# Scores and transposes of the first groups through eight PSUM banks, a third query buffer, and a new order for an attention kernel with two layers behind it

## The chip, the cores and the metric

One core of one Trainium2 chip. The time is device microseconds (us) of one execution, the median of several. Beside it stands the span of a profiled execution, from its first to its last instruction. Engines: PE is TensorE (PEld its weight loads), DVE VectorE, ACT ScalarE, POOL GpSimd, SP the engine that issues DMAs.

## The reference, cut to what matters

```python
def _attn_ref(q, k, v, n_sink, window):          # (2, 8, 768, 64) float32, n_sink 4, window 128
    scores = scale * np.matmul(q, k.transpose(0, 1, 3, 2))
    keep = is_sink | in_window                   # 4 first keys, and the last 128
    scores = np.where(keep, scores, -1000000000.0)
    a = np.exp(scores - np.max(scores, axis=-1, keepdims=True))
    a = a / (np.sum(a, axis=-1, keepdims=True) + 1e-09)
    return np.matmul(a, v)

x = attention as (1536, 512)
h = x @ w_in                                     # (512, 2048)
g = np.where(h > 0.0, h, np.exp(np.minimum(h, 0.0)) - 1.0)
x = g @ w_out                                    # (2048, 512)
h = x @ w2_in
g = h - np.tanh(h)
return g @ w2_out
```

## The kernel before

**Order.** The program is first written down as a list of operations with their dependences (class `Plan`), then `schedule` (line 269) simulates the engines with modelled costs and picks for each engine a fixed order; `emit` issues it (line 400, which is the line that nearly all instructions show; line 168 is the same for bundles of matmuls). What an engine takes next is set by a rank: for kinds of operations in the table `DUE`, a due time that is linear in a counter; else the length of the path to the end. `PICK` says for kinds of elementwise operations which engines may do them. `BONUS` makes PE prefer to stay in its tiling mode, `MARGIN` lets an operation wait for a faster engine. When the model finds PE without work, before the first matmul of an output step, it puts in filler matmuls on constants (line 591), which keep PE running and compute nothing.

**Attention.** 12 chunks of 128 queries (6 per batch), each in two groups of 4 heads, so 24 groups g. Per group: `scores` twice, each a bundle of matmuls for two heads into two PSUM banks of `b_sc` (banks 0, 1); DVE reads each bank, adds the mask, and writes the scores and their least value (CUSTOM_DVE_ANT_0), ACT takes the exponential and the sum. `norm`: DVE adds 1e-9 and inverts, then four multiplications of 128, 256 or 264 columns (first chunk of a batch, second, others) on the engine that `PICK` says. `sink_T` and `pair_T` transpose on PE into `b_tu` (banks 2, 3), and a copy brings the result to SBUF. After two groups `PV` multiplies by the values into a bank of `b_tu` and writes x as a sum of two float32r parts, `xhi` and `xlo`. A ring of `AB = 3` buffers holds the scores of three groups, one of `QB = 2` the queries of two chunks, and `NS = 3` slots the keys.

**Layers.** Each weight tile is read as float64, narrowed by integer operations on ACT, DVE and POOL (`narrow`: absolute value, a min/max, a shift, two bit operations), and split in two float32r parts. Eight weight tiles are held. Phase 0 runs over 6 blocks of 256 tokens with 3 weight tiles: `mlp_in` (12 matmuls into a bank of `b_hA`, banks 4, 5), an elementwise part, `mlp_out` (banks 6, 7 of `b_yA`). Phase 0 runs beside the attention, as the blocks of x come. The five later phases work with 512 columns and all eight banks, when the attention is over.

**Dependences on banks.** A later user of a PSUM bank waits for the earlier ones in the order of the list; the list has all of the attention first, then the layers' steps.

Of the kernel before, what the change touches and what calls it, by code (L numbers as in the profile page):

```python
# [7 lines left out]
F32 = mybir.dt.float32  # L8
# [8 lines left out]
P = 128  # L17
# [24 lines left out]
class Plan:  # L42
# [13 lines left out]
    TOP = 640e3  # L56
    WINDOW, ENOUGH, IDLE = 3413.3, 3100.0, (109.2, 256.0)
    SWITCH = (196.0, 95.0)
    BONUS, MARGIN = 2030.75, 5520.33

    HOLD = {}
    DUE = {
# [4 lines left out]
    }  # L67

    PICK = {
        ("T", "copy", 128, True): ("ACT",), ("ew", "copy", 256, False): ("ACT", "DVE"),  # L70
        ("norm", "tensor_scalar", 264, False): ("DVE",), ("T", "copy", 64, False): ("POOL",),
        ("late w", "tensor_scalar", 512, False): ("DVE",), ("late ew", "tensor_tensor", 512, False): ("DVE",),
        ("T", "tensor_tensor", 32, False): ("DVE",), ("late ew", "copy", 512, False): ("ACT",),
        ("c", "tensor_copy", 128, False): ("POOL",), ("w", "tensor_scalar", 512, False): ("POOL",),
        ("late w", "tensor_tensor", 512, False): ("DVE",), ("late out", "copy", 512, True): ("DVE",),
        ("w", "tensor_tensor", 512, False): ("DVE",), ("T", "copy", 256, True): ("ACT",),
        ("late w", "copy", 512, False): ("DVE",), ("T", "copy", 512, True): ("ACT",),
        ("out", "copy", 512, True): ("ACT",), ("x", "copy", 512, True): ("ACT", "DVE"),
        ("norm", "tensor_scalar", 128, False): ("DVE",), ("norm", "tensor_scalar", 256, False): ("DVE", "POOL"),
        ("w", "copy", 512, False): ("ACT", "DVE", "POOL"), ("z", "copy", 512, False): ("DVE",),  # L80
        ("ew", "tensor_tensor", 256, False): ("DVE",),
    }

    def __init__(self, tc):
# [75 lines left out]
    def many(self, products):  # L160

        if self.live:
            raise AssertionError
        eng = self.T.eng

        def real():
            for kw in products:
                eng.matmul(**kw)  # L168

        mode, = {self.tiling(kw) for kw in products}  # L170
        cost = sum(self.matmul_cost(kw) for kw in products)
        work = sum(self.work_of(kw) for kw in products)
        ins, outs = [], []
        for kw in products:
            ins += [kw["lhsT"], kw["rhs"]]
            outs.append(kw["out"])
        self.enter({"PE": (cost, real, False)}, ins, outs, (), {}, "PE", False, work, mode)

    def either(self, *recs, **kw):

        if self.live:
            return getattr(recs[0][0].eng, recs[0][1])(**kw)
        cols = 1
        for k in kw["out"].shape[1:]:
            cols *= k
        psum = any(getattr(a, "space", None) == PSUM for a in kw.values())
        key = (self.tag[0], recs[1][1], cols, psum)
        pick = self.PICK.get(key)
        self.choice = key
        self.record([(r.key, m, getattr(r.eng, m)) for r, m in recs if pick is None or r.key in pick], (), kw, True)  # L190
        self.choice = None

    choice = None
# [1 line left out]
    def record(self, ways, args, kw, any_=False):  # L195
        named = list(kw.items()) + [("out" if i == 0 else f"in{i}", a) for i, a in enumerate(args)]
        named = [(k, a) for k, a in named if hasattr(a, "tensor")]
        outs = [a for k, a in named if k in ("out", "accum_out")]
        ins = [a for k, a in named if k not in ("out", "accum_out")]
        there = [a for a in ins if "DRAM" not in str(a.space)]  # L200
        eng = ways[0][0]
        costs = {}
        psum = any(a.space == PSUM for a in there + outs)
        for e, method, real in ways:
            if e == "DMA":
                size = 1
                for k in outs[0].shape[1:]:
                    size *= k
                costs[e] = (max(600.0, 0.0111 * size * outs[0].shape[0]), real, False)
            else:  # L210

                lock = (e == "DVE" and not psum) or (e == "POOL" and method == "tensor_tensor")
                costs[e] = (self.cost(e, method, outs[0], there, kw), real, lock)
        pe = eng == "PE"
        self.enter(costs, there, outs, args, kw, eng, any_, self.work_of(kw) if pe else 0.0, self.tiling(kw) if pe else 0)
# [53 lines left out]
    def schedule(self):  # L269
        from bisect import insort  # L270
        from heapq import heappush, heappop
        ops, N, engs = self.ops, len(self.ops), self.ENGINES
        succ, rank = self.ranks()
        ways = [list(o[1].items()) for o in ops]
        left = [len(o[2]) for o in ops]
        free = dict.fromkeys(engs, self.START)
        wait = {e: [] for e in engs}
# [10 lines left out]

        def offer(n):
            for k, (e, _) in enumerate(ways[n]):  # L290
                heappush(wait[e], (at[n][e] + late[n], 3 * n + k))

        for n in range(N):
            if not left[n]:
                offer(n)
        order = []
        stop, tiled, count = False, 0, 0
        win = [self.WINDOW, 2.0, 0.0, 0.0]

        def clock(t):  # L300
# [11 lines left out]
        while count < N:  # L312
# [21 lines left out]
            if e == "PE":  # L334
                top = -1e18
                for i, (v, q) in enumerate(r[:40]):
                    v = -v + (self.BONUS if ops[q // 3][7] == tiled else 0.0)
                    if v > top + 1e-9:
                        top, pick = v, i
            elif e in held:  # L340

                until = held[other[e]]
                for i, (v, q) in enumerate(r):
                    if until <= t or not ways[q // 3][q % 3][1][2]:
                        pick = i
                        break
                else:
                    s = max(t, until)
# [2 lines left out]
            c, real, lock = ways[n][q % 3][1]  # L351
            earlier = False
            for f, (cf, _, lf) in ways[n]:
                if f != e:
                    sf = max(free[f], at[n][f] + late[n])
                    if lf:
                        sf = max(sf, held[other[f]])
                    earlier = earlier or sf + cf + self.MARGIN < s + c
            if earlier:
# [5 lines left out]
            if e == "PE":  # L365

                stop = stop or (ops[n][5] or "-")[0] == "out"
                while not stop and free[e] + clock(free[e]) * self.IDLE[0] <= t:
                    order.append((free[e], -1, self.idle))
                    free[e] += run(free[e], *self.IDLE)  # L370
                    tiled = 0
                s = max(s, free[e])
                x = 0.0
                if ops[n][7] != tiled:
                    x = (self.SWITCH[1] if tiled else 0.0) + (self.SWITCH[0] if ops[n][7] else 0.0)
                    tiled = ops[n][7]
                c = run(s, c + x, ops[n][6])
            free[e] = s + c
            if lock:
                held[e] = s + c  # L380
            order.append((s, n, real))
            for k in succ[n]:
                for f in at[k]:
# [20 lines left out]
def tile_sink_attention__two_mlps(  # L404
# [119 lines left out]

    gsA = Ring("att", (2, 256), F32R, 3)

    KS, NS, QB, VB, AB, TB = 144, 3, 2, 4, 3, 8
    r_q = Ring("att", (HP, P), F32, QB)
    slots = carve("att", (NS, HP, KS))
    r_a = Ring("att", (4, KW), F32, AB)  # L530
# [14 lines left out]
    t1s += [carve("late", (DM,), U32) for _ in range(3)]  # L545
    eB, gsB = Ring("late", (512,), F32, 3), Ring("late", (2, 512), F32R, 2)
    b_sc, b_tu, b_hA, b_yA = Banks(0, 1), Banks(2, 3), Banks(4, 5), Banks(6, 7)
    b_hB, b_hE, b_yB = Banks(0, 1, 2, 3), Banks(0, 1, 2), Banks(4, 5, 6, 7)
    small = const.tile([P, 16], F32, name="small")

# [118 lines left out]
    def split_sinks(b, r):  # L669

        if b == 0:
            vsink[0] = r_vsink()
        z = vsink[b] = vsink[0]
        copy(z[0:3 * S4], r[0:3 * S4])
        rows = slice(2 * S4, 3 * S4)
        sub(V_, z[rows], r[rows], z[rows].bitcast(F32))

    a_t, aT_t, aS_t = {}, {}, {}

# [8 lines left out]
    def scores(g, pr):  # L688
# [7 lines left out]
        n = width(i)  # L696
        mm, S = [], []
        for rows in (top, bot):
            bk = b_sc(512)
            S.append(bk)  # L700
            if i == 0:
                K, to = slots[rows, o, p, 0:P], bk[:, 0:P]
# [33 lines left out]
    def sink_T(g):  # L736
# [5 lines left out]
        s = r_as()  # L742
        copy(s[:, 1:3], a.unsqueeze(1).to_broadcast([P, 2, 4, MAXSINK]))
        sub(None, s[:, 0], a, s[:, 1].bitcast(F32))
        tr = b_tu(P)[0:3 * S4]
        T_.matmul(
            out=tr, lhsT=s.rearrange("p a h s -> p (a h s)").bitcast(F32), rhs=ident,
            is_transpose=True, start=True, stop=True,
# [4 lines left out]
    def pair_T(g, pr):  # L753
# [2 lines left out]
        c = g // 2  # L756
        i = c % NI
        a = a_t[g]
        tr = b_tu(2, 2, P)
        c0, c1 = slice(0, P), slice(P, 2 * P) if i == 1 else s1  # L760
        cols = (c1, c0) if i != 1 and c % NS == 0 else (c0, c1)
        n0 = 1 if i == 0 else 0
# [8 lines left out]
    def PV(c):  # L771

        plan.tag = ("pv", 2 * c + 1)
        b, i = divmod(c, NI)
        U = b_tu(4, P)
        if i >= 2:

            plan.many([
# [412 lines left out]
```

## Time and profile before

| what | us |
|---|---|
| median of 3 runs | 637.05 (636.72 to 637.23) |
| the profiled execution | 636.36 |
| its span | 634.6 |
| PE busy, share of the span | 627.1, 99% |
| DVE busy | 431.9, 68% |
| ACT busy | 278.6, 44% |
| POOL busy | 30.8, 5% |
| granted TensorE clock, mean | 0.998 |

Busy time of PE includes the filler matmuls. Busy shares are means over stages that differ: DVE's 68% is nearly full in the first quarter and half idle later. The profiled execution took 636.36 us, 1.8 us more than its span, and 0.7 us less than the median.

### The profile page before, as it was taken

How to read it: one execution, taken by the hardware profiler on the slowest of the kernel's cores; microseconds unless marked ns; L12 is line 12 of the kernel's file. 1: busy time of each engine (PE TensorE's matmuls, PEld its weight loads, DVE VectorE, ACT ScalarE, POOL GpSimd, SP SyncE). 2: the span in 40 equal slices, each digit the busy share in tenths (PEclk: the TensorE clock that was granted, in tenths of full speed). 3: DMA queues.
4: the chain of work that ended last, by engine and by line, in shares of the span. 5: the costliest groups of instructions: out<-in, count | busy, mean ns of one | idle time of the engine just before them, and what ended most of it. 6: DMA issues, size and time to landing. Idle time of an engine off the chain costs nothing.

```text
span 634.6 us, 9256 instructions
## 1 busy us (share of the span) xinstructions
PE 627.1 (99%) x3430; PEld 514.5 (81%) x3430; DVE 431.9 (68%) x1061; ACT 278.6 (44%) x615; POOL 30.8 (5%) x41
## 2 busy tenths in 40 slices
PE   9999999999999999999999999999999999999996
PEld 6677877899888888888888888888888888888885
DVE  6999999999824479943459998367974553423232
ACT  5788887875533345533445453223422222222220
POOL 3631020100000000000000000000000000000000
PEclk9999999999999999999999999999999999999999
DMA  6543444345500122430012243011220000001012
GB/s 212 172 162 121 130 162 133 99 139 165 165 1 0 35 66 68 132 100 0 1 34 67 74 158 116 17 40 59 70 66 2 2 0 1 0 1 66 2 66 72
DMA packets 22005, 47.21 MB, mean 74 GB/s; under 512 B 2240, under 2 KB 9408, under 8 KB 21952
## 3 DMA queue, kind: packets, MB, share of 16 engines
q1 hardware_dynamic: 21952, 46.54, 23.7%
q8 instruction: 29, 0.48, 0.3%
q14 instruction: 24, 0.20, 0.1%
HBM read 43.39 MB, written 3.15 MB: 73 GB/s over the span
## 4 chain that ended last, share of the span: by engine, by line
PE 82%; DVE 13%; DMA 2%; POOL 1%; SPq 1%; issue 1%; ACT 0%; DVEq 0%; POOLq 0%
PE bank L400 79%; DVE arena L400 7%; DVE t L400 3%; PE bank L168 2%; DVE arena_r L400 1%; DVE w L400 1%; DMA raw<-in_moe_w_in_dram 1%; DVE xlo L400 1%; SPq L400 1%; POOL t L400 1%; DMA arena<-in_kq_dram 1%; DVE sm_all L400 1%; POOL arena_r L400 0%; DVE xhi L400 0%; ACT arena L400 0%
## 5 line engine op out<-in xcount | busy, mean ns | idle before, releaser
L400 PE MATMUL bank<-xhi,w 128*128 128x512 f32 (+1 forms) x840 | 250.7, 373 | 0.0
L400 PEld LDWEIGHTS bank<-xhi,w 128*128 128x128 f32 x840 | 154.6, 188 | 28.7 <-issue 1.6
L400 PE MATMUL bank<-arena_r,w 128*128 128x512 f32 (+1 forms) x684 | 158.8, 358 | 0.0
L400 PE MATMUL bank<-w,arena_r 128*128 128x512 f32 (+1 forms) x594 | 154.4, 383 | 0.0
L400 PE MATMUL bank<-xlo,w 128*128 128x512 f32 (+1 forms) x420 | 148.2, 373 | 0.0
L400 ACT CAST arena_r<-arena 128x512 fp32r<-128x512 f32 (+1 forms) x96 | 57.9, 603 | 194.2 <-PE bank L400 192.1
L400 PEld LDWEIGHTS bank<-arena_r,w 128*128 128x128 f32 x684 | 116.5, 189 | 19.3 <-issue 0.9
L400 DVE TENSOR_TENSOR arena_r<-arena,arena_r 128x512 fp32r<-128x512 f32 (+3 forms) x123 | 71.4, 582 | 89.1 <-PE bank L400 42.8
L400 PEld LDWEIGHTS bank<-w,arena_r 128*128 128x128 f32 x594 | 109.3, 188 | 22.1
L400 ACT ACTIVATE arena<-bank 128x512 f32<-128x512 f32 (+1 forms) x105 | 57.9, 560 | 101.0 <-PE bank L400 97.5
L400 PEld LDWEIGHTS bank<-xlo,w 128*128 128x128 f32 x420 | 79.0, 188 | 14.6 <-issue 1.1
L400 DVE TENSOR_TENSOR arena<-bank,arena 128x512 f32<-128x512 f32 (+1 forms) x65 | 42.4, 677 | 38.2 <-ACT arena L400 31.8
L168 PE MATMUL bank<-arena 128*64 128x128 f32 (+3 forms) x544 | 55.3, 327 | 0.5 <-DVE nm_all L400 0.4
L400 ACT ACTIVATE arena<-arena,nm_all 128x264 f32<-128x264 f32 (+2 forms) x96 | 46.8, 491 | 15.6 <-DVE nm_all L400 14.9
L400 DVE SCALAR_TENSOR_TENSOR arena<-arena,bank 128x512 f32<-128x512 f32 (+1 forms) x57 | 33.9, 596 | 22.0 <-ACT arena L400 22.0
L400 ACT ACTIVATE arena<-arena 128x512 f32<-128x512 f32 (+1 forms) x73 | 42.5, 587 | 8.1 <-DVE w L400 6.6
L168 PEld LDWEIGHTS bank<-arena 128*64 128x64 f32 (+1 forms) x544 | 34.7, 154 | 11.1 <-issue 4.3
L400 DVE SCALAR_TENSOR_TENSOR t<-raw,t 128x512 uint32<-128x512 uint32 x54 | 37.2, 688 | 0.2
L400 DVE CUSTOM_DVE_ANT_0 arena<-bank,arena 128x264 f32<-128x264 f32 (+2 forms) x96 | 35.1, 398 | 0.4 <-PE bank L168 0.2
L400 ACT COPY arena<-bank 128x512 f32<-128x512 f32 (+1 forms) x52 | 27.5, 544 | 3.2 <-PE bank L168 3.2
L400 DVE TENSOR_SCALAR t<-t 128x512 f32<-128x512 f32 (+1 forms) x64 | 27.1, 425 | 2.0 <-POOL t L400 1.1
L168 PE MATMUL bank<-ident,arena 128*128 128x128 f32 x176 | 27.6, 281 | 0.2 <-DVE xlo L400 0.2
(67 smaller groups left out, 408.8 us busy)
## 6 DMA issues: line engine op xcount, KB each, us to landing
raw<-in_moe_w_in_dram SPq DMA_DIRECT2D x20, 512.0 KB, 3.7
raw<-in_moe_w_out_dram SPq DMA_DIRECT2D x20, 512.0 KB, 3.8
arena<-in_moe_w_in_dram SPq DMA_DIRECT2D x12, 512.0 KB, 3.6
arena<-in_moe_w_out_dram SPq DMA_DIRECT2D x12, 512.0 KB, 3.6
arena<-in_kq_dram SPq DMA_DIRECT2D x22, 256.0 KB, 3.4
arena<-in_v_dram SPq DMA_DIRECT2D x12, 256.0 KB, 3.4
out_dram<-part SPq DMA_DIRECT2D x8, 256.0 KB, 2.2
out_dram<-arena SPq DMA_DIRECT2D x3, 256.0 KB, 2.5
```

What stands on the lines that cost most here:

```text
L168: eng.matmul(**kw)
L400: real(*self.ops[n][3], **self.ops[n][4])
```

## The change

Scores of the groups 0 to 5 rotate through banks 0, 1, 4, 5, and transposes and `PV` of these groups through banks 2, 3, 6. There is a third query buffer. The due times, `BONUS`, `MARGIN` and the engines in `PICK` are other ones, so the order of all engines is other. In the model of `schedule`, DVE copies and multiplications in SBUF now take up to twice as long while a POOL instruction runs beside them (the bit of `lock` worth 2). The split of the sinks (`split_sinks`) may be subtracted on POOL. `PICK` is applied within `schedule` and no longer when the operation is written down.

```diff
-    BONUS, MARGIN = 2030.75, 5520.33
+    BONUS, MARGIN = 6316.39, 7595.77
     DUE = {
-        "c": (-2246.58, 70.043), "score": (-751.72, 15.580), "ew": (169.97, 10.912), "lkq": (-825.49, 29.089),
-        "norm": (31.65, 0.041), "lw": (-323.61, 20.339), "w": (-51.16, 95.951), "end": (1519.18, -106.955),
-        "x": (-392.68, 18.828), "pv": (89.97, 9.529), "in": (76.02, 17.601), "out": (207.21, 11.159),
-        "kq": (-189.70, 22.587), "T": (23.13, 10.469), "ok": (444.48, 24.538), "lv": (48.72, 3.987),
+        "c": (-3936.74, 120.076), "score": (-1284.21, 29.194), "norm": (-1209.56, 18.705), "end": (2560.24, 6.088),
+        "x": (120.74, 7.962), "in": (-185.94, -9.701), "ew": (-192.46, 32.491), "out": (321.10, 12.351),
+        "lkq": (-932.85, 18.488), "lw": (-583.73, -27.211), "w": (291.28, 0.591), "T": (-407.36, 10.770),
+        "pv": (-505.98, 13.124), "kq": (-360.38, 77.393), "lv": (130.54, 6.759), "ok": (106.81, -109.242),
+        "late ew": (46.59, 5.616),
     }
     PICK = {
-        ("T", "copy", 128, True): ("ACT",), ("ew", "copy", 256, False): ("ACT", "DVE"),
-        ("norm", "tensor_scalar", 264, False): ("DVE",), ("T", "copy", 64, False): ("POOL",),
-        ("late w", "tensor_scalar", 512, False): ("DVE",), ("late ew", "tensor_tensor", 512, False): ("DVE",),
-        ("T", "tensor_tensor", 32, False): ("DVE",), ("late ew", "copy", 512, False): ("ACT",),
-        ("c", "tensor_copy", 128, False): ("POOL",), ("w", "tensor_scalar", 512, False): ("POOL",),
-        ("late w", "tensor_tensor", 512, False): ("DVE",), ("late out", "copy", 512, True): ("DVE",),
-        ("w", "tensor_tensor", 512, False): ("DVE",), ("T", "copy", 256, True): ("ACT",),
-        ("late w", "copy", 512, False): ("DVE",), ("T", "copy", 512, True): ("ACT",),
-        ("out", "copy", 512, True): ("ACT",), ("x", "copy", 512, True): ("ACT", "DVE"),
-        ("norm", "tensor_scalar", 128, False): ("DVE",), ("norm", "tensor_scalar", 256, False): ("DVE", "POOL"),
-        ("w", "copy", 512, False): ("ACT", "DVE", "POOL"), ("z", "copy", 512, False): ("DVE",),
-        ("ew", "tensor_tensor", 256, False): ("DVE",),
+        ("T", "copy", 128, True): ("ACT", "DVE"), ("ew", "copy", 256, False): ("DVE",),
+        ("norm", "tensor_scalar", 264, False): ("POOL",), ("T", "copy", 64, False): ("ACT", "POOL"),
+        ("late w", "tensor_scalar", 512, False): ("DVE",),
+        ("late ew", "tensor_tensor", 512, False): ("DVE", "POOL"), ("T", "tensor_tensor", 32, False): ("DVE",),
+        ("late ew", "copy", 512, False): ("DVE",), ("c", "tensor_copy", 128, False): ("POOL",),
+        ("w", "tensor_scalar", 512, False): ("DVE",), ("late w", "tensor_tensor", 512, False): ("DVE",),
+        ("late out", "copy", 512, True): ("ACT",), ("w", "tensor_tensor", 512, False): ("DVE", "POOL"),
+        ("T", "copy", 256, True): ("DVE",), ("late w", "copy", 512, False): ("ACT", "DVE"),
+        ("T", "copy", 512, True): ("ACT",), ("out", "copy", 512, True): ("ACT", "DVE"),
+        ("x", "copy", 512, True): ("ACT", "DVE"), ("norm", "tensor_scalar", 128, False): ("POOL",),
+        ("norm", "tensor_scalar", 256, False): ("DVE",), ("w", "copy", 512, False): ("ACT", "DVE", "POOL"),
+        ("z", "copy", 512, False): ("DVE", "POOL"), ("ew", "tensor_tensor", 256, False): ("DVE",),
+        ("z", "tensor_tensor", 512, False): ("DVE",),
     }
...
-                lock = (e == "DVE" and not psum) or (e == "POOL" and method == "tensor_tensor")
+                lock = int(e == "DVE" and not psum) or int(e == "POOL" and method == "tensor_tensor")
+                if lock and method in ("tensor_copy", "tensor_scalar"):
+                    lock = 3
...
+            if lock & 2:
+                c += min(c, max(0.0, beside - s))
             free[e] = s + c
-            if lock:
+            if lock & 1:
                 held[e] = s + c
+            elif e == "POOL":
+                beside = s + c
...
-    KS, NS, QB, VB, AB, TB = 144, 3, 2, 4, 3, 8
+    KS, NS, QB, VB, AB, TB = 144, 3, 3, 4, 3, 8
...
     b_sc, b_tu, b_hA, b_yA = Banks(0, 1), Banks(2, 3), Banks(4, 5), Banks(6, 7)
+    b_sc0, b_tu0 = Banks(0, 1, 4, 5), Banks(2, 3, 6)
...
-        sub(V_, z[rows], r[rows], z[rows].bitcast(F32))
+        sub(None, z[rows], r[rows], z[rows].bitcast(F32))
...
-            bk = b_sc(512)
+            bk = (b_sc0 if g < 6 else b_sc)(512)
...
-        tr = b_tu(P)[0:3 * S4]
+        tr = (b_tu0 if g < 6 else b_tu)(P)[0:3 * S4]
...
-        tr = b_tu(2, 2, P)
+        tr = (b_tu0 if g < 6 else b_tu)(2, 2, P)
...
-        U = b_tu(4, P)
+        U = (b_tu0 if c < 3 else b_tu)(4, P)
```

## Rows read from the trace of the kernel before

**Rows 1.** Stages: PE, PEld, DVE, ACT, POOL busy us (count), clock, DMA share, GB/s.

```profile
0.00:32.00 32.00, 30.70 (x243) 19.82 (x244) 27.12 (x120) 20.37 (x64) 15.52 (x20) 1.00 0.63 193
32.00:109.00 77.00, 76.82 (x667) 60.13 (x666) 75.72 (x300) 63.79 (x201) 13.32 (x17) 1.00 0.44 139
...
200.00:560.00 360.00, 360.00 (x1590) 298.11 (x1589) 234.11 (x422) 126.78 (x211) 0.00 (x0) 1.00 0.16 49
```

**Rows 2.** The chain that ended last: start us, us, what.

```profile
12.17 2.05 POOL t L400
...
108.39 0.61 DVE xlo L400
109.04 0.66 PE bank L168 x4
...
559.87 68.76 PE bank L400 x320
```

**Rows 3.** Stages to 60 us, filler matmuls of line 591 alone: the sum.

```profile
sum 60.00, PE 17.61 PEld 10.27; mean PE 3.52 PEld 2.05
```

**Rows 4.** Timeline, 8 to 33 us: start us, us, engine, line, operation.

```profile
8.89 0.49 PE L168 MATMUL bank<-arena 64*128 64x128 f32 x4
...
15.67 1.73 PE L168 MATMUL bank<-arena 128*64 128x128 f32 x20
...
16.69 0.30 PEld L168 LDWEIGHTS bank<-arena 64*128 64x128 f32 x4 [0.17 <-DVE nm_all L400]
...
27.48 0.73 PE L168 MATMUL bank<-arena 64*128 64x272 f32 x4
...
29.11 0.43 DVE L400 CUSTOM_DVE_ANT_0 arena<-bank,arena 128x264 f32<-128x264 f32 x1
...
29.23 2.63 PE L168 MATMUL bank<-arena 128*64 128x128 f32 x36
...
31.88 0.50 PE L400 MATMUL bank<-xhi,w 128*128 128x256 f32 x2
```

**Rows 5.** Timeline of SP's DMA issues: the queries of chunk 2.

```profile
9.45 0.33 SPq L400 DMA_DIRECT2D arena<-in_kq_dram  x1
```

**Rows 6.** Groups by shape, DVE to 157 us, then POOL: count, busy us, mean ns.

```profile
L400 DVE TENSOR_SCALAR arena<-arena,sm_all 128x264 f32<-128x264 f32 x64 | 19.0, 349 | 0.0
L400 DVE TENSOR_SCALAR t<-t 128x512 uint32<-128x512 uint32 x19 | 8.4, 444 | 1.1 <-POOL t L400 1.1
L400 DVE TENSOR_SCALAR t<-t 128x512 f32<-128x512 f32 x13 | 5.4, 412 | 0.4 <-ACT t L400 0.4
L400 DVE CAST w<-t 128x512 fp32r<-128x512 f32 x11 | 4.5, 412 | 0.0
L400 DVE TENSOR_SCALAR arena<-arena,sm_all 128x128 f32<-128x128 f32 x16 | 3.8, 300 | 0.0
L400 DVE TENSOR_SCALAR arena<-arena,sm_all 128x256 f32<-128x256 f32 x9 | 3.6, 431 | 0.0
L400 DVE CAST arena_r<-arena 128x256 fp32r<-128x256 f32 x9 | 2.5, 282 | 0.0
L400 DVE TENSOR_TENSOR arena<-bank,arena 128x256 f32<-128x256 f32 x2 | 0.8, 418 | 0.6 <-PE bank L400 0.6
L400 POOL TENSOR_SCALAR t<-t 128x512 f32<-128x512 f32 x6 | 12.2, 2026 | 9.6 <-ACT t L400 9.5
L400 POOL TENSOR_SCALAR arena<-arena,sm_all 128x256 f32<-128x256 f32 x7 | 7.3, 1053 | 19.1 <-ACT arena L400 13.8 <-DVE sm_all L400 5.3
```

**Rows 7.** Timeline: DVE beside a POOL multiplication of weights.

```profile
12.17 3.98 POOL L400 TENSOR_SCALAR t<-t 128x512 f32<-128x512 f32 x2 [6.50 <-ACT t L400]
...
14.25 0.88 DVE L400 TENSOR_SCALAR t<-t 128x512 uint32<-128x512 uint32 x1 [0.46 <-POOL t L400]
...
15.16 0.69 DVE L400 SCALAR_TENSOR_TENSOR t<-raw,t 128x512 uint32<-128x512 uint32 x1
```

**Rows 8.** Timeline: the last addition.

```profile
628.65 0.69 DVE L400 TENSOR_TENSOR arena<-bank,arena 128x512 f32<-128x512 f32 x1 [0.44 <-PE bank L400]
```

More of the change, by code (lines that the diff above doesn't have):

```diff
@@ L176, in many @@
             outs.append(kw["out"])
-        self.enter({"PE": (cost, real, False)}, ins, outs, (), {}, "PE", False, work, mode)
+        self.enter({"PE": (cost, real, 0)}, ins, outs, (), {}, "PE", False, work, mode)
     def either(self, *recs, **kw):
@@ L187, in either @@
         key = (self.tag[0], recs[1][1], cols, psum)
-        pick = self.PICK.get(key)
         self.choice = key
-        self.record([(r.key, m, getattr(r.eng, m)) for r, m in recs if pick is None or r.key in pick], (), kw, True)
+        self.record([(r.key, m, getattr(r.eng, m)) for r, m in recs], (), kw, True)
         self.choice = None
@@ L208, in record @@
                     size *= k
-                costs[e] = (max(600.0, 0.0111 * size * outs[0].shape[0]), real, False)
+                costs[e] = (max(600.0, 0.0111 * size * outs[0].shape[0]), real, 0)
             else:
-                lock = (e == "DVE" and not psum) or (e == "POOL" and method == "tensor_tensor")
+                lock = int(e == "DVE" and not psum) or int(e == "POOL" and method == "tensor_tensor")
+                if lock and method in ("tensor_copy", "tensor_scalar"):
+                    lock = 3
                 costs[e] = (self.cost(e, method, outs[0], there, kw), real, lock)
@@ L274, in schedule @@
         ways = [list(o[1].items()) for o in ops]
+        may = [self.PICK.get(o[8], engs) for o in ops]
         left = [len(o[2]) for o in ops]
@@ L290, in offer @@
             for k, (e, _) in enumerate(ways[n]):
-                heappush(wait[e], (at[n][e] + late[n], 3 * n + k))
+                if e in may[n]:
+                    heappush(wait[e], (at[n][e] + late[n], 3 * n + k))
         for n in range(N):
@@ L296, in schedule @@
         order = []
-        stop, tiled, count = False, 0, 0
+        stop, tiled, count, beside = False, 0, 0, 0.0
         win = [self.WINDOW, 2.0, 0.0, 0.0]
@@ L343, in schedule @@
                 for i, (v, q) in enumerate(r):
-                    if until <= t or not ways[q // 3][q % 3][1][2]:
+                    if until <= t or not ways[q // 3][q % 3][1][2] & 1:
                         pick = i
@@ L353, in schedule @@
             for f, (cf, _, lf) in ways[n]:
-                if f != e:
+                if f != e and f in may[n]:
                     sf = max(free[f], at[n][f] + late[n])
-                    if lf:
+                    if lf & 1:
                         sf = max(sf, held[other[f]])
```

## Prediction, made before the changed kernel ran

> **What bounds the kernel now.** I read the stages first. From 200 to 560 us PE is busy without a break, 1590 matmuls in 360.00 us or 0.226 us each, with DVE at 234.11 of 360 [rows 1]. Nothing can be won there, since no matmul goes away. From 32 to 109 us PE shows 76.82 of 77 us busy, and so does DVE with 75.72: two engines are full at once [rows 1]. The chain of waits decides between them. It runs through DVE work until 108.39 us, and from 109.04 us through PE alone to the end of the matmuls [rows 2]. So PE sets the pace from 109 us on, and what counts is how much of PE's fixed work is behind it by then. That is lessened by the time in which PE had nothing to do. Busy PE hides it, because the order fills such time with matmuls on constants: 17.61 us of them, all before 41 us [rows 3]. This is the whole store of time from which a better order of the early part can take, apart from short stalls of PE between 32 and 109 us.
>
> Then I read the timeline before the first layer matmul, at 31.88 us [rows 4]. From the last scores of chunk 0 (8.89 us) to its product with the values (15.67 us) it takes 6.8 us; the same way in chunk 1 goes from 16.69 to 29.23 us, 12.5 us [rows 4]. The tiles are twice as wide, but 5.7 us more is mostly a queue: DVE takes scores of later groups and weights in between. The scores at 16.69 us had waited for DVE to read the banks, as the wait on that row says [rows 4].
>
> **The change part by part.**
>
> *More banks for scores, transposes and products.* Two bundles of scores, not one, can stand in PSUM, so PE runs ahead and DVE chooses what to read. It adds no instruction. What it takes away is a round trip per bundle, but DVE is the engine that is short: it is busy 27.12 of the first 32 us [rows 1], and its 4.9 idle us include the start, when nothing is loaded. The gain must come from order: chunk 1 first, groups 4 and 5 after it. Bound above: the 5.7 us by which chunk 1 was slower. Bound below: nothing, as the new banks are also taken from the layers. Step 0 writes its first result to bank 4, and the last scores to use bank 4 are those of group 5, which PE made at 27.48 us and DVE finished reading at 29.54 us (29.11 plus 0.43) [rows 4]. With DVE's order unchanged the first layer matmul could come 2.3 us earlier and no more. I take 3 us, half of the first bound; PE's filler shrinks by as much. Waiting behind step 0 on PE would be step 1 and the transposes of chunk 2, which can go first.
>
> *The narrowing of the first weights.* Six min/max operations go from POOL (2.026 us each) to DVE (0.412 us) [rows 6]. The first of these POOL operations lies on the chain, 2.05 us [rows 2]. This is why I do not take less than 3 us above: 1.6 us come off the way to the first weights alone. On DVE it costs 2.5 us, counted below.
>
> *Third query buffer.* The queries of chunk 2 were requested at 9.45 us, after the last scores of chunk 0 had begun at 8.89 us [rows 4, 5]; now they go at once. Nothing gained: they are used only after chunk 1, whose last scores are at 16.69 us. For later chunks the key slot stays the limit, which is free only when the scores two chunks before are done, the same condition as for two query buffers. If that cover went, the worst is SP's own 0.33 us per issue [rows 5], put ahead of weight loads.
>
> *Who does what.* DVE loses 64 multiplications of 264 columns (19.0 us) and 16 of 128 (3.8 us), 22.8 us in all. It gains 7 of 256 columns at 0.431 (3.0 us), the 6 min/max (2.5), 9 copies of the elementwise part at 0.282 (2.5), and 8 copies out of PSUM of 256 columns, which I price as the addition of that shape, 0.418 (3.3) [rows 6]. That is 11.3 us, so DVE is 11.5 us lighter before any side effect. Copies that may now go either way (of weights, of outputs) I leave out: they move both ways between ACT and DVE.
>
> The side effect is on the same engine. While POOL worked from 12.17 to 16.15 us, a DVE operation of one SBUF input took 0.88 us [rows 7]; its mean is 0.444, lifted by such cases [rows 6]. The next one, with two inputs, took its usual 0.69 us under the same POOL operation [rows 7]. So the first kind doubles beside POOL. POOL will run 64 multiplications at 1.053 × 264/256 = 1.086 us and 16 at about half of 1.053, together 78 us [rows 6]. The stretch for it runs from 8.9 us to the end of the attention, which I put near 135 us from the 24 groups (an estimate: the chain at 109 us still holds score bundles). That is a share of 0.61. The operations that would double: 8.4 + 5.4 + 4.5 + 2.5 + 3.6 us from before and 3.0 + 2.5 + 2.5 us added, 32.4 us [rows 6]. At chance that costs 19.8 us; at the other end nothing, if the order keeps them apart. The new order counts the doubling, but with DVE full it has little room to dodge. I take a share of 0.35: 11.3 us, which cancels the 11.5 us. Net 0, between −11.5 and +8.3 us on DVE; while the chain lies on DVE (109 of 135 us) the end moves by 0.81 of that, −9.3 to +6.7 us.
>
> *The rule that speaks against it.* In the trace the DVE operation started at 14.25 us and ended at 15.13, before POOL was done at 16.15 us [rows 7]: it ran slowly and did not wait. The Trainium skill, page "SBUF — State Buffer", section "Who interferes with whom", has it harder: the two engines share a port pair as an exclusive lock, and the one that comes second is blocked until the other's instruction is over, also when a DVE instruction has two SBUF inputs. By the row the term is the one above; by the rule it is that of the last rival below. The trace does not agree with the rule here, on both points: 0.88 us is less than the wait, and 0.69 us is no wait.
>
> *Later stages.* Copies of the elementwise part (512 columns) go from ACT to DVE, about 0.41 us each [rows 6], one per step of 24 matmuls or 5.4 us. DVE has 126 idle us of 360 there [rows 1], so this is costed at nothing; some subtractions may go to POOL, where 512 columns took 2.026 us in another operation [rows 6], and even that is under a step. If the cover went, PE would stall by the excess in each step; I see none.
>
> *The end.* The last piece of the output is now one of 256 columns, since the due time rises with the piece: the last addition takes 0.418 instead of 0.69 us [rows 6, 8], −0.3 us. Not below: −0.7, if it vanished; above: nothing, if the narrower write lands that much later.
>
> **Sum.** −3.0 (early) + 0 (DVE) + 0 (late) − 0.3 (end) = −3.3 us. The profiled execution took 636.36 us for its span of 634.6 us; it would take 633.1. It stands 0.7 us below the median of 637.05, so the forecast for the median is 633.8 us.
>
> **The rivals.**
>
> *DVE gets its relief.* The order keeps DVE's copies off POOL's instructions, share 0.1: DVE is 8.3 us lighter, the end 6.7 us earlier, with the early gain 627 us. For it: nothing else is on POOL after 40 us (13.32 us busy from 32 to 109 [rows 1]). Against it: POOL would be busy three fifths of the time. Chance 0.10.
>
> *The wait moves to bank 4.* Step 0 stands behind group 5's scores, and weights and x come no sooner, so the filler changes place only: 637 us. For it: DVE's 75.72 of 77 us [rows 1], an engine that cannot do the same work faster for another order. Chance 0.17.
>
> *POOL makes DVE slow, and the end is later.* At the chance share of 0.61 DVE carries 8.3 us more; the end moves by 6.7 us, 640.5 with the early gain and 643.8 without. Beside it a group's four multiplications take 4.3 us on POOL instead of 1.4 on DVE, which delays transposes. It decides from a share of 0.48 on, where 0.81 × (32.4 × share − 11.5) passes 3.3 us. For it: the 0.88 us [rows 7]. Against it: the share needs DVE's copies to fall on POOL's work nearly at random. Chance 0.27.
>
> *DVE is blocked outright.* Each DVE operation on SBUF that meets a POOL multiplication waits half of its 1.086 us; with some 150 such operations to 135 us (an estimate from the counts of such groups, doubled for those with two inputs [rows 6]) and a share of 0.61 this is 50 us, by 0.81 a time near 677 us. The Trainium skill's lock, named above, is this case. The 0.69 us [rows 7] speaks against it. Chance 0.02.
>
> **How the numbers follow.** A change under 0.2% (1.3 us) can hardly be told from none here. My forecast, 632 to 635.5 us, has 0.44. Faster: 0.44 + 0.10 = 0.54. Within 0.2%: 0.17. Slower: 0.27 + 0.02 = 0.29. The range runs from 629.5, halfway into the second case, to 641.0 us, past the third rival with its early gain; left out are some 0.05 below and 0.12 above.
>
> **What the profile will show.** Right: first layer matmul at 28 to 30 us; filler near 14.6 us; POOL busy about 80 us more; DVE operations of one SBUF input between 0.42 and 0.88 us; the chain on DVE until 105 to 108 us, then PE alone. Wrong: PE stalls or gaps after 200 us; the chain through POOL's multiplications; the first layer matmul at 32 us or later; DVE's busy time to 157 us unchanged but the switch to PE later than 109 us.

## The result, and the profile after

The changed kernel took 629.79 us (median of 4, 629.20 to 630.62), the kernel before, measured beside it, 636.99 us (636.72 to 637.23): ratio 0.9891, 95% interval 0.9879 to 0.9902. It is 7.2 us faster. The forecast was 633.8 us, 3.3 us faster; the range, 629.5 to 641.0 us, just holds the time, but the gain is 2.2 times the forecast one. The profiled execution took 630.28 us for a span of 628.4 us, so the two profiles differ by 6.2 us of span, and that is what the views below can account for.

The page of the changed kernel: busy time, share of the span and instructions of each engine, and the shares of the chain that ended last.

```profile
PE 621.5 (99%) x3394; PEld 511.5 (81%) x3394; DVE 437.6 (70%) x1005; ACT 252.5 (40%) x570; POOL 147.0 (23%) x142
...
PE 98%; POOL 1%; DVE 0%; issue 0%; POOLq 0%
```

POOL went from 31 to 147 us busy. The chain is PE's nearly throughout. Its stages, columns as in [rows 1]:

```profile
0.00:32.00 32.00, 31.22 (x242) 20.37 (x243) 26.79 (x128) 23.77 (x77) 16.14 (x29) 1.00 0.65 195
32.00:109.00 77.00, 77.00 (x686) 62.32 (x684) 72.57 (x264) 64.95 (x196) 55.44 (x59) 1.00 0.47 143
...
200.00:560.00 360.00, 360.00 (x1590) 298.20 (x1589) 241.10 (x407) 111.70 (x190) 51.45 (x34) 1.00 0.16 49
```

From 32 to 109 us PE has no gap left (77.00 of 77), and DVE now has 4.4 us to spare. After 200 us PE does the same 1590 matmuls in the same 360.00 us. The clock is 1.00, as before. The whole stretch to 157 us, by which the attention is over, shows DVE at 150.23 us in the kernel before and at 144.80 us after (the first line is before, the second after):

```profile
0.00:157.00 157.00, 155.47 (x1334) 124.10 (x1335) 150.23 (x559) 119.09 (x350) 30.83 (x41) 1.00 0.48 151
```
```profile
0.00:157.00 157.00, 156.04 (x1320) 125.69 (x1321) 144.80 (x509) 121.83 (x349) 88.61 (x103) 1.00 0.49 150
```

The chain of waits after, in order of time (start us, us, what), against [rows 2]:

```profile
0.76 4.64 PE bank L601 x21
...
121.83 0.95 POOL arena L409
125.32 2.46 POOL arena L409 x2
128.11 2.07 POOL arena L409 x2
...
137.15 485.28 PE bank L409 x2203
```

The chain lies on PE from the first microsecond, not from 109 us on. Up to 34.2 us, where the last filler ends, it runs through filler too, and there it does not tell what held the real work up. The filler of line 601 (L591 before), as in [rows 3]:

```profile
sum 60.00, PE 13.84 PEld 7.51; mean PE 2.77 PEld 1.50
```

That is 86 filler matmuls where there were 122, 3.8 us less. The timeline of PE, as in [rows 4]: two pairs of score bundles that follow each other (of 256 and of 272 columns), the product of chunk 1 with the values, the first layer matmul.

```profile
9.68 1.13 PE L170 MATMUL bank<-arena 64*128 64x256 f32 x8
...
14.66 1.19 PE L170 MATMUL bank<-arena 64*128 64x272 f32 x8
...
24.11 2.63 PE L170 MATMUL bank<-arena 128*64 128x128 f32 x36
...
27.18 0.36 PE L409 MATMUL bank<-xhi,w 128*128 128x256 f32 x1
```

The product of chunk 1 begins 5.1 us earlier, the first layer matmul 4.7 us earlier, at 27.18 instead of 31.88 us. Two bundles of 256 columns back to back take 1.13 us, where one alone takes 0.70 us (below, in the run that splits the pairs). These lengths overlap with what follows; from the start of the first to the start of the next thing on PE a pair costs 1.07 us, and a bundle alone 0.63 (worked out from the traces of the change and of that run).

**Where the 6.2 us came from.** Adding up, for each matmul, the time from its start to the start of the next one on PE (worked out from the two traces): filler 17.1 to 13.0 us, −4.1; score bundles 30.9 to 29.0, −1.9; transposes 21.8 to 21.1, −0.7; all the rest +0.5 or so. That is the −6.1 us by which the last matmul starts earlier.

### The profile page after: what moved, and what is told of

The parts are those of the page before. It is cut to its first block, busy times and chain, and to the rows that moved or that the text cites. A ratio compares the mean times of both kernels' runs of the same rounds, so it can differ in the third digit from the quotient of the medians.

```text
span 628.4 us, 9220 instructions
## 1 busy us (share of the span) xinstructions
PE 621.5 (99%) x3394; PEld 511.5 (81%) x3394; DVE 437.6 (70%) x1005; ACT 252.5 (40%) x570; POOL 147.0 (23%) x142
## 4 chain that ended last, share of the span: by engine, by line
PE 98%; POOL 1%; DVE 0%; issue 0%; POOLq 0%
PE bank L409 84%; PE bank L170 11%; PE bank L601 2%; POOL arena L409 1%; DVE arena L409 0%; DVE arena_r L409 0%; DVE t L409 0%; DVE sm_all L409 0%; POOL arena_r L409 0%; DVE bad L409 0%; POOLq L409 0%
## 5 line engine op out<-in xcount | busy, mean ns | idle before, releaser
L409 PE MATMUL bank<-xhi,w 128*128 128x512 f32 (+1 forms) x840 | 246.6, 373 | 0.0
L409 POOL TENSOR_TENSOR arena_r<-arena,arena_r 128x512 fp32r<-128x512 f32 x40 | 59.9, 1498 | 410.5 <-DVE arena_r L409 202.7
L409 PE MATMUL bank<-xlo,w 128*128 128x512 f32 (+1 forms) x420 | 143.7, 373 | 0.0
L409 DVE CAST arena_r<-arena 128x512 fp32r<-128x512 f32 (+1 forms) x105 | 43.1, 411 | 86.8 <-PE bank L409 86.4
L409 POOL TENSOR_SCALAR arena<-arena,sm_all 128x264 f32<-128x264 f32 (+1 forms) x80 | 81.2, 1030 | 34.8 <-DVE sm_all L409 13.4
L409 DVE TENSOR_TENSOR arena_r<-arena,arena_r 128x512 fp32r<-128x512 f32 (+2 forms) x83 | 44.9, 544 | 29.8 <-PE bank L409 26.2
L170 PE MATMUL bank<-arena 128*64 128x128 f32 (+3 forms) x544 | 53.1, 326 | 0.0
L409 DVE SCALAR_TENSOR_TENSOR t<-raw,t 128x512 uint32<-128x512 uint32 x54 | 40.1, 742 | 0.2
L409 ACT CAST w<-arena 128x512 fp32r<-128x512 f32 x25 | 15.5, 621 | 49.8 <-PE bank L409 40.7
```

The source lines that it names most:

```text
L409: real(*self.ops[n][3], **self.ops[n][4])
```

## The experiments

All were timed beside the kernel before, which took 636.67 to 636.97 us in these runs. Three theories stood against each other from the start: that the wider **banks** carry the gain, that DVE's **relief** by POOL does, or that the **order** does, which the planner makes out of due times and modelled costs and which needs the other two only as far as it uses them. After the first runs the expectations speak of two others: "together" (banks and engines are needed at once, old due times will do) and "fragile" (due times fit one set of banks and engines). Two questions came later: what POOL's presence costs, and whether the shorter time of paired score bundles is a cause.

| run | median us | ratio to before, 95% interval | span us | filler us | PE idle to 157 us | first layer matmul us |
|---|---|---|---|---|---|---|
| before | 636.99 | 1 | 634.6 | 17.6 | 1.5 | 31.88 |
| after | 629.79 | 0.9891 [0.9879, 0.9902] | 628.4 | 13.8 | 1.0 | 27.18 |
| e1, banks off | 640.84 | 1.0062 [1.0049, 1.0075] | 639.9 | 23.4 | 1.9 | 33.65 |
| e12, scores' banks only | 633.60 | 0.9952 [0.9938, 0.9965] | 631.7 | 18.4 | 0.8 | 30.07 |
| e13, transposes' banks only | 641.04 | 1.0068 [1.0054, 1.0081] | 638.6 | 22.3 | 1.5 | 33.27 |
| e5, before + banks | 636.38 | 0.9995 [0.9986, 1.0003] | 634.7 | 16.9 | 3.2 | 31.41 |
| e6, before + engines | 639.06 | 1.0037 [1.0023, 1.0051] | 636.8 | 19.4 | 2.1 | 31.33 |
| e9, before + banks + engines | 640.20 | 1.0058 [1.0045, 1.0072] | 637.4 | 16.9 | 6.0 | 30.51 |
| e2, multiplications on DVE, planned anew | 636.33 | 0.9997 [0.9986, 1.0007] | 633.4 | 14.1 | 5.0 | 28.80 |
| e10, the same in after's order | 635.34 | 0.9980 [0.9971, 0.9989] | 633.1 | 13.6 | 3.1 | 27.79 |
| e15, multiplications left out | 629.62 | 0.9878 [0.9862, 0.9895] | 628.1 | 14.0 | 0.8 | 27.39 |
| e8, model without the doubling | 636.10 | 0.9987 [0.9978, 0.9996] | 635.2 | 13.8 | 4.9 | 27.73 |
| e11, a fifth of the doubling | 635.83 | 0.9986 [0.9977, 0.9995] | 633.7 | 14.4 | 5.4 | 27.08 |
| e3, two query buffers | 629.77 | 0.9892 [0.9877, 0.9906] | 628.2 | 13.5 | 0.9 | 26.62 |
| e4, old `BONUS` | 630.01 | 0.9897 [0.9882, 0.9912] | 627.5 | 13.8 | 0.9 | 26.97 |
| e16, pairs split | 630.24 | 0.9890 [0.9874, 0.9907] | 629.8 | 14.5 | 0.9 | 28.40 |

(PE idle is 157 us less PE's busy time in that stretch. Filler and idle are two forms in which PE does nothing useful. Their sum follows the span: the span less the sum lies between 612.5 and 616.5 us in all sixteen rows.)

### Banks

**e1: the changed kernel without the wider banks, planned anew.**

```diff
-    b_sc0, b_tu0 = Banks(0, 1, 4, 5), Banks(2, 3, 6)
+    b_sc0, b_tu0 = b_sc, b_tu
```

> The changed kernel with banks 0, 1 and 2, 3 alone for all groups, as before; engines, due times and query buffers stay. Theory 'relief' (the time comes from DVE, which gave its multiplications to POOL and is hardly slowed by them): 629 to 631 us, at most 1 us over the changed kernel's 629.8. Rival 'banks' (the time comes from PE running bundles of scores ahead and in pairs): 634 us or more, filler matmuls back at 110 or more. Rival 'order' (due times and BONUS alone): 629 to 631 us, as relief.

640.84 us, 11 us slower than the change. The filler of its stretch to 60 us:

```profile
sum 60.00, PE 23.41 PEld 13.03; mean PE 4.68 PEld 2.61
```

The new due times with the old banks wait more than the old kernel did: the loss is 9.6 us of filler, and the first layer matmul comes at 33.65 us. **e12 and e13** give back one half each: `b_tu0 = b_tu` (e12: scores wide, transposes narrow) and `b_sc0 = b_sc` (e13, the other way round).

> The changed kernel with the wider rotation for scores alone (banks 0, 1, 4, 5); transposes and products in banks 2, 3. Theory 'scores ahead': 630 to 633 us. Rival 'the third bank of transposes and products counts as much': 636 us or more.

> The changed kernel with the wider rotation for transposes and products alone (banks 2, 3, 6); scores in banks 0, 1. Theory 'scores ahead': 638 to 642 us, as without any of the banks. Rival 'third bank': 631 to 634 us.

Scores' banks alone keep 3.2 of the 7.2 us (633.60 us, between the ranges of the two theories, so the third bank counts for about half). Transposes' banks alone keep nothing: 641.04 us, where e1 is. So the scores' banks come first, and the transposes' third bank is worth some 4 us only on top of them.

**e5: the kernel before with the wider banks alone** (the lines of the diff that name `b_sc0` and `b_tu0`, old due times and engines).

> The kernel before with the wider rotation of banks for the first groups alone; its due times, BONUS and engines stay. Theory 'relief': 636 to 638 us, no change, since DVE is as full as it was. Rival 'banks': 632 to 635 us. Rival 'order': 636 to 638 us.

636.38 us, no difference. Necessary for the new order, then (e1), but not sufficient. This is the time that the rival of the wait at bank 4 named, but its cause is not shown: the first layer matmul comes at 31.41 us right behind transposes, and DVE is as full as it was, 76.09 of the 77 us from 32 to 109.

### Engines

**e6: the kernel before with the new `PICK` alone**, and **e9: with banks and new `PICK`, old due times.**

> The kernel before with the engines of the new table alone (multiplications of 264 and 128 columns on POOL, the rest of the table too); two banks each, old due times. Theory 'together' (DVE's time and the PSUM banks each hold the early part back, so neither alone gives anything): 635 to 638 us. Rival 'relief alone': 631 to 634 us, DVE some 5 us lighter up to 157 us and the end earlier by as much. Rival 'fragile' (due times fit one set of engines and banks; any other loses): 638 us or more.

> The kernel before with both the banks and the new table of engines; old due times and BONUS. Theory 'together': 630 to 633.5 us, most of the gain without new due times. Rival 'fragile': 635 us or more. This is the run that tells the two apart.

Engines alone 2.4 us slower, both together 3.5 us slower. The theory that banks and engines do it together fell here: what is missing in e9 is the order (and the third query buffer, which e3 finds worth nothing). Its stage from 32 to 109 us:

```profile
32.00:109.00 77.00, 72.73 (x629) 57.84 (x629) 73.29 (x260) 60.27 (x191) 57.21 (x53) 1.00 0.49 150
```

PE idles for 4.3 of these 77 us.

**e2: the changed kernel with the multiplications of weights back on DVE**, planned anew.

```diff
-        ("norm", "tensor_scalar", 264, False): ("POOL",),
+        ("norm", "tensor_scalar", 264, False): ("DVE",),
-        ("norm", "tensor_scalar", 128, False): ("POOL",),
+        ("norm", "tensor_scalar", 128, False): ("DVE",),
```

> The changed kernel with the multiplications of 264 and 128 columns back on DVE; banks, due times and the rest stay. Theory 'relief': DVE is some 20 us heavier up to 157 us, the chain lies on DVE again, 634 to 638 us. Rival 'banks' and rival 'order': 629 to 631.5 us, since the store of filler was cut by the banks or the order, and PE, not DVE, sets the pace.

**e10: the same with after's order kept word for word**; only the engine that the 80 multiplications are issued on differs.

```diff
+            if e == "POOL" and ops[n][5] and ops[n][5][0] == "norm":
+                real = ops[n][1]["DVE"][1]
             order.append((s, n, real))
```

> The changed kernel's order word for word, but the 80 multiplications that it gives to POOL are issued on DVE at the same places. Theory 'relief' (DVE's 22.8 us are needed in this order): DVE would have to do 72.6 + 16 to 18 us in the 77 us from 32 to 109, so 638 us or more. Rival 'order alone' (DVE has room to take them, since it is idle 4 us there and POOL's 4 us per group become 1.4): 629 to 633 us.

636.33 and 635.34 us: without the relief nearly all, or 5.5 of 7.2 us, of the gain is gone. (e10 lies between the ranges of its two theories.) e10 from 32 to 109 us:

```profile
32.00:109.00 77.00, 75.36 (x656) 59.68 (x655) 76.69 (x302) 63.17 (x190) 4.22 (x8) 1.00 0.46 139
```

DVE is full again (76.69 of 77) and PE has gaps again. PE's matmuls and their order, filler included, are the same in both, so this relief is shown to be worth 5.5 us in this order.

**e15: what POOL's multiplications cost.** They are left out, so that those weights are not divided by their sums; order and everything else stay.

```diff
-            order.append((s, n, real))
+            if e == "POOL" and ops[n][5] and ops[n][5][0] == "norm":
+                pass
+            else:
+                order.append((s, n, real))
```

> The changed kernel in its own order, with the 80 multiplications of weights by the inverse sum on POOL left out: those rows of the attention are not normalised. The work and its tax on DVE are gone at once, so the run prices all that POOL costs here. Theory of the record (POOL beside DVE is dear: 11.3 us on DVE to 157 us, 0.81 of it on the end): about 9 us earlier, near 621 us. Theory after the runs so far (the tax is 4 to 5 us on DVE, and PE alone sets the pace of this order): PE has no gap between 32 and 109 us to give back, so the time stays within 1 us of the changed kernel, 629 to 630 us, while DVE's busy time to 157 us falls by 4 to 5 us.

629.62 us: no difference. Three groups of DVE to 157 us by shape, first with the multiplications (changed kernel), then without (e15); the last two numbers before the idle time are busy us and mean ns:

```profile
L409 DVE SCALAR_TENSOR_TENSOR t<-raw,t 128x512 uint32<-128x512 uint32 x38 | 28.0, 737 | 0.1
...
L409 DVE TENSOR_SCALAR t<-t 128x512 uint32<-128x512 uint32 x19 | 8.5, 448 | 0.1
L409 DVE TENSOR_SCALAR t<-t 128x512 f32<-128x512 f32 x19 | 8.5, 447 | 0.2
```
```profile
L412 DVE SCALAR_TENSOR_TENSOR t<-raw,t 128x512 uint32<-128x512 uint32 x38 | 27.2, 715 | 0.1
...
L412 DVE TENSOR_SCALAR t<-t 128x512 uint32<-128x512 uint32 x19 | 8.0, 422 | 0.1
L412 DVE TENSOR_SCALAR t<-t 128x512 f32<-128x512 f32 x19 | 8.0, 422 | 0.4 <-ACT t L412 0.2
```

And e15's stage to 157 us:

```profile
0.00:157.00 157.00, 156.22 (x1322) 126.14 (x1323) 141.66 (x510) 121.18 (x349) 8.45 (x23) 1.00 0.51 151
```

DVE's total falls from 144.80 to 141.66 us: the tax of POOL on DVE is 3.1 us, 3 to 6% on these operations (4 to 5 us had been expected), and none of it reaches the end in this order. The run could hardly have shown more: PE does the same 3394 matmuls in the same order, the 86 filler matmuls among them, so that only PE's gaps, 1.0 us to 157 us, could close. What an order made without this tax could save is not shown. Note the chain of waits shown above: it names POOL's multiplications between 121.83 and 130.2 us. They release the transposes at 130.22 us, but PE was busy with other matmuls meanwhile (27.83 of the 28 us from 109 to 137 us):

```profile
109.00:137.00 28.00, 27.83 (x269) 24.71 (x267) 25.47 (x80) 20.27 (x54) 15.44 (x16) 1.00 0.38 118
```

Without them PE has the same matmuls to do in the same order, and nothing is gained.

### Order

**e8: the planner's model without the doubling of DVE beside POOL; e11: with a fifth of it.** Instructions, banks, engines allowed and due times are those of the change. The two differ from it in the order that comes out, and where a choice was open, in the engine.

```diff
             if lock & 2:
-                c += min(c, max(0.0, beside - s))
+                c += 0.2 * min(c, max(0.0, beside - s))
```

> The changed kernel without the doubling of DVE's time beside POOL in the model of its order; instructions, engines and due times are the same, only the order moves a little. Theory 'together': 629 to 631.5 us, since the trace shows DVE's operations slowed by some 15% beside POOL and not doubled, so the term hardly matters. Rival 'fragile': 633 us or more.

> The changed kernel, its order made with a fifth of the doubling (about what the trace of the changed kernel shows of DVE beside POOL's multiplications); same instructions, engines, banks and due times. Theory 'order' (any other order of the same work, not found with its own search, has PE wait): 633 to 637 us. Rival 'the size in the model counts' (an order made with the measured size is as good or better): 628 to 631 us.

636.10 and 635.83 us: 6 us of the 7.2 are lost. The main theory's 629 to 631.5 us for e8 missed. e8's waits of PE from 32 to 157 us (in total, times, longest):

```profile
PE bank L170 <- ACT arena L407: 2.0, 1, 2.0
PE bank L407 <- DVE arena_r L407: 0.7, 1, 0.7
```

The longest of them on the timeline:

```profile
66.30 0.63 PE L170 MATMUL bank<-ident,arena 128*128 128x128 f32 x4 [2.01 <-ACT arena L407]
```

The first layer matmul is as early as in the change (27.73 us), the filler as little (13.79 us), but PE stands idle 4.9 us behind it: here a transpose waits 2.01 us for exponentials. An early start that the next 100 us cannot feed is lost again. The fifth is nearer to the measured tax than the doubling, and it gives no better order. So the doubling does not help by being true; the due times fit the order that it leads to.

### The rest

**e3: `QB` 2 instead of 3; e4: `BONUS` 2030.75 instead of 6316.39.**

> The changed kernel with two query buffers. All theories: 629 to 631 us. The key slots hold the same loads back, so no more than 1 us is lost; over 632 us the third buffer would be a part of the gain that I had costed at nothing.

> The changed kernel with BONUS back at 2030.75, all else as changed. Theory 'together' with a part for the mode switches of PE (bundles of scores in pairs took 1.9 us less of PE): 630.5 to 632.5 us if BONUS makes the pairs, 629.5 to 630.5 if the banks do. Rival 'fragile': 633 us or more.

629.77 and 630.01 us. The third query buffer is worth nothing. With the old `BONUS` the same order came out, so e4 is a second measurement of the change.

**e16: the four pairs of score bundles split.** One of the kernel's own filler matmuls moves between the two bundles of groups 1 to 4, all before 17 us.

```diff
         order.sort(key=lambda x: x[:2])
+        pe = [i for i, x in enumerate(order) if x[1] < 0 or "PE" in ops[x[1]][1]]
+        for a, b in zip(pe, pe[1:]):
+            if all(order[i][1] >= 0 and (ops[order[i][1]][5] or "-")[0] == "score" for i in (a, b)):
+                f = next((i for i in pe if i > b and order[i][1] < 0), None)
+                if f is not None:
+                    fill = (order[b][0],) + order[f][1:]
+                    order[b + 1:f + 1] = order[b + 1:f]
+                    order.insert(b, fill)
```

> The changed kernel with one of its own filler matmuls moved between the two bundles of scores that follow each other on PE, in four groups (1 to 4), all before 15 us. Work and count of every kind stay. Theory that the shorter time of two bundles back to back is itself part of the gain: four times some 0.3 us, 1.1 us later, near 631 us. Theory that this is only bookkeeping (PE waits for DVE and ACT at that time, and the filler would fill the difference): 629.8 us, within 0.4, and the first layer matmul where it was, near 27.2 us.

```profile
10.04 0.70 PE L170 MATMUL bank<-arena 64*128 64x256 f32 x4
10.87 0.70 PE L170 MATMUL bank<-arena 64*128 64x256 f32 x4
```

The bundles are back at 0.70 us each, and in the profiled execution the first layer matmul comes at 28.40 us, 1.2 us later, and the span is 1.4 us longer. The timed runs don't confirm that: 630.24 us, 0.45 us above the change, at a ratio of 0.9890 against 0.9891, and the profiled execution was the longest of its four (631.63 us). This stays open between nothing and 1.4 us.

## Why the prediction was half right

**Right.** The direction; the store from which the gain comes (PE's time without work before 41 us), for 4.3 of the 6.2 us; the first layer matmul earlier (27.18 us, the forecast was 28 to 30); filler at 13.8 us (14.6); no harm after 200 us; nothing for the third query buffer; DVE not blocked by POOL's multiplications. The size was wrong: 7.2 us instead of 3.3. The rival in which DVE gets its relief was the one nearest to the truth, at 627 us and with a chance of 0.10.

**The step that failed first: "the side effect", 11.3 us of DVE.** One row of 0.88 us [rows 7] was taken as the rule for a class of operations, which would double whenever they meet POOL. Nor was it beside a multiplication of attention weights, as the caption of [rows 7] has it: POOL's operation there (`t<-t`, 512 columns) is a min/max of the narrowing. The mean of the class went from 422 ns without POOL's multiplications to 448 with them. The tax on everything DVE does to 157 us is 3.1 us (e15), not 11.3. It is small because the operations don't double, not because the order keeps them apart: of the 38 operations `t<-t` of one input in the change, 16 lie almost wholly beside multiplications on POOL, a share of 0.42 where the forecast took 0.35. They took 482 ns in the mean (414 to 626), the 16 that meet no POOL instruction 418 (worked out from the trace). A timeline beside four multiplications of 264 columns:

```profile
20.83 3.95 POOL L409 TENSOR_SCALAR arena<-arena,sm_all 128x264 f32<-128x264 f32 x4 [5.83 <-ACT arena L409]
```
```profile
21.87 0.91 DVE L409 SCALAR_TENSOR_TENSOR t<-raw,t 128x512 uint32<-128x512 uint32 x1
22.70 0.43 DVE L409 TENSOR_SCALAR t<-t 128x512 f32<-128x512 f32 x1
```

The operation with one input, which was to double, took its usual 0.43 us; the one with two, which was to go undisturbed, took 0.91. So "net 0 on DVE" was wrong: DVE is 5.4 us lighter to 157 us (some 2 us more without the later work that the earlier order brings into this stretch, worked out from the traces), and has 4.4 us to spare from 32 to 109 us, where it had been full. What POOL's taking the multiplications is worth was measured by e10, 5.5 us. By the forecast's own factor of 0.81 the 5.4 us are 4.4 at the end, and the sum would have come to 633.8 − 4.4 = 629.4 us. That this is near the measured time is luck: the factor stands for a chain on DVE, which the change ended, and with the tax alone put right (11.5 − 3.1 = 8.4 us) it gives 627.0 us.

**The early term, −3.0 us.** Mis-sized: filler and idle of PE fell by 4.3 us in the profile, and the first layer matmul came 4.7 us earlier. It was bounded by what bank 4 allows "with DVE's order unchanged", and DVE's order did not stay. The half by which it was cut had no row behind it.

**PE's own time was taken as fixed.** The sum has no term for it. Score bundles and transposes cost 2.5 us less from start to start. A part is the four pairs, some 0.8 us (e16 leaves open whether it counts at the end). A part is single bundles that got shorter: of the 32 bundles of 272 columns, 0.73 us each, seven took 0.77 to 1.07 us in the kernel before, none over 0.76 in the change, and again seven 0.77 to 1.29 in e10, with a full DVE. One of each (before, then e10):

```profile
24.66 1.07 PE L168 MATMUL bank<-arena 64*128 64x272 f32 x4
```
```profile
111.95 1.29 PE L170 MATMUL bank<-arena 64*128 64x272 f32 x4
```

I read that as a stop in their middle for a bank that DVE had not read; the rows give only the length.

**The chain.** It was to run on DVE until 105 to 108 us. It left DVE altogether. From 32 to 157 us PE has 0.2 us of gaps, so DVE no longer holds it up there. The chain also shows a sign that the forecast called wrong, POOL's multiplications, for 5.5 us between 121.83 and 130.2 us; e15, without them, ends no earlier. POOL is busy 116 us more and not about 80: 58 us of them come after 157 us, where the forecast had left the subtractions open.

**The end, −0.3 us.** The last addition did get shorter, but the span ends 5.95 us after its start in both kernels (628.4 − 622.45; before, 634.6 − 628.65 [rows 8]):

```profile
622.45 0.42 DVE L409 TENSOR_TENSOR arena<-bank,arena 128x256 f32<-128x256 f32 x1 [0.29 <-PE bank L409]
```

**What the parts are worth.** Not additive. Each one alone on the kernel before gives nothing or a loss (e5, e6, e9), and each one taken out of the change costs 5.5 to 11 us (e1, e2, e8, e10, e11; some 4 us for the transposes' banks, e12), save the query buffer and `BONUS`. Only runs that keep the order fixed (e10, e15, e16) price a single part; in the others the planner's answer to the part is in the time too. Not run: the new due times alone, with the old banks and engines; `MARGIN` alone; the other new entries of `PICK`, the min/max of the narrowing among them. Why exactly this order leaves PE no gap was not taken further apart than e8's waits, and stays open.

## What to carry to other kernels

Where two engines are full at once, moving work from one of them to an idle engine can pay, in an order made for it, even though the idle engine is three times slower per operation (1105 ns against 349 [rows 6]) and disturbs the first; price the disturbance from a mean over many operations beside the very operation that moves, not from one row beside another. An order made for given banks and engines is a part of the change: judge a resource with the order made for it, and price it by taking it out with the order kept. A run that keeps the order can show a loss, but no gain beyond the gaps of the bounding engine, since the filler stays in. Time without work on the bounding engine hides in two places, filler and gaps, and a change that shrinks one can fill the other.

## What the runs showed of the hardware

**POOL beside DVE depends on POOL's operation.** POOL's multiplications of 264 columns took 1105 ns in the mean beside DVE's work, and cost the groups of DVE's operations above 3 to 6%:

```profile
L409 POOL TENSOR_SCALAR arena<-arena,sm_all 128x264 f32<-128x264 f32 x64 | 69.8, 1105 | 28.6 <-ACT arena L409 9.9 <-PE bank L170 7.5 <-DVE sm_all L409 7.3
```

POOL's subtractions of two SBUF inputs (512 columns), which the change brought to the later phases, are another matter. POOL and DVE at 360 us:

```profile
360.24 1.67 POOL L409 TENSOR_TENSOR arena_r<-arena,arena_r 128x512 fp32r<-128x512 f32 x1 [3.20 <-DVE arena_r L409]
```
```profile
360.67 1.78 DVE L409 SCALAR_TENSOR_TENSOR t<-arena,t 128x512 uint32<-128x512 uint32 x1
```

DVE's operation, 0.69 us by itself, ends at 362.45 us, 0.54 us after POOL's at 361.91, as if most of its work were done after POOL's. In eight more places from 237 to 390 us a DVE operation took 1.78 or 1.79 us. Here the exclusive lock of the Trainium skill (page "SBUF — State Buffer", section "Who interferes with whom") agrees with the trace. For POOL's multiplications it doesn't: 21 operations of two inputs (`t<-raw,t`, 512 columns) that lay almost wholly beside them took 0.68 to 0.91 us, 0.72 in the mean, against 0.68 for the nine that met no POOL instruction. PE did not notice the subtractions: 360.00 of 360 us busy after 200 us.
